# Decode attention beside an MLP: the extra rows of w4 by plain DMAs and h's columns made on chip

## The chip, the cores and the metric

One core of a Trainium2 chip runs the whole program. The metric is the device time of one execution in microseconds (us); lower is better. Before the change it is 403.15 us, the median of 3 runs (402.7 to 404.05).

## The reference

One token (S = 1, D = 1024) goes through a layer norm, then through two branches that are added: attention of 32 query heads over a cache of 65,536 keys in 4 groups, and a mixer with an MLP.

```python
q = (xn @ wq)                                  # 32 heads of 128
p = softmax(q . k * 128 ** -0.5)               # k, v: 4 groups x 65536 x 128, 8 heads share a group
o = (p . v) @ wo
h  = gelu(layernorm(xn) @ w1)
hs = concatenate(shifted quarters of h) @ w2   # S = 1: every shifted quarter is zero
x1 = xn + hs
h2 = gelu(layernorm(x1) @ w3) @ w4             # w3: 1024 x 3584, w4: 3584 x 1024
out = x0 + attention + x1 + h2                 # x0: the token before the layer norm
```

All inputs are bf16. K and V together are 134 MB, and the program reads 170 MB in all.

## The kernel before

**Slots.** Everything large is read into one of three slots of 64 KB per partition, in the order of a list: wq; then K and V of a group in two halves each (a half is 8.4 MB, 64 KB on each of 128 partitions); w3 behind the first K and V; behind the third group a slot with w1, w4's first piece (12 of w4's 25 row blocks) and "x4"; at the end wo, and a last slot with w2 and w4's pieces of 9, 3 and 1 blocks. `ensure(i + LOOKAHEAD)` issues a slot two ahead of the one that is computed on, from SP, as soon as the slot's last user three places earlier is done.

**w4's rows.** w4 has 3584 = 28 x 128 rows. 25 x 128 of them are laid out evenly, 25 rows on each partition (FB = 25). The other 384 rows are "x4" and are not spread evenly: the table XP lists ranges of partitions that get four rows each (eleven ranges, 70 partitions, 280 rows) and ranges that get one row each (five ranges, 104 partitions, 104 rows). Partitions outside of the ranges have zeros there. On a partition the four-row column block comes first (4 x 1024 values, 8 KB), then the one-row block (2 KB).

**How the x4 rows come.** `fill_x_row` (L138) works out, on DVE, a table of one row number for each partition and each of the two blocks; partitions out of the ranges get a number over the bound. `gather_rows` (L155) issues an indirect DMA from GpSimd that reads the row for each partition and skips those over the bound. In `issue`, x4 is zeroed by GpSimd (L167) and filled by two such gathers.

**How h comes.** `compute_w3` (L375) makes h (3584 values) as eight rows of 448 in PSUM, applies gelu on ACT into `hrow` (partitions 0, 32, 64 and 96, two rows each), and calls `bounce` (L360): GpSimd writes the rows to a scratch in DRAM (L363), reads them back as 25 columns with one value for each partition (L367), and, as x4 needs h's values in the very places of its rows, gathers five more columns by the same row tables (L371, L156).

**The product.** `compute_w4(0)` and `compute_x4` add up w4's first piece and x4 in one PSUM tile (`pair_acc`, L526); the result joins the output row through `row_acc` (L230). Each engine has one queue and works it off in order. SP has the queue q1, GpSimd's DMAs are q0, and the sixteen DMA engines serve both.

**K and V.** `compute_K` (L426) transposes a half of K in place on DVE (L435), makes scores on PE (L439), the maxima on DVE, and the exponentials on ACT (L462); `compute_V` (L479) multiplies on PE (L486) and rescales on DVE (L494). The output is copied on ACT (L417) and written from SP (L418).

Of the kernel before, what the change touches and what calls it, by code (L numbers as in the profile page):

```python
# [8 lines left out]
BF16 = mybir.dt.bfloat16  # L9
F32 = mybir.dt.float32  # L10
ACTF = mybir.ActivationFunctionType
ALU = mybir.AluOpType
# [11 lines left out]
XR = (4, 1)  # L24
XP = (((0, 15), (16, 20), (28, 44), (48, 52), (60, 70), (72, 74), (76, 78), (80, 82), (84, 87), (92, 100), (124, 128)),
      ((0, 20), (28, 52), (60, 88), (92, 120), (124, 128)))
NO_ROW = 4096
HEAD = 96


# [1 line left out]
def kernel(  # L32
# [14 lines left out]
    nc = tc.nc  # L47
    P = 128
# [7 lines left out]
    F = B_w3.shape[1]  # L56
    DC = D // P
    FC = F // P
    NOUT = A_wo.shape[1]
# [4 lines left out]
    FW = F // 8  # L64
# [7 lines left out]
    const = ctx.enter_context(tc.tile_pool(name="const", bufs=1))  # L72
# [3 lines left out]
    tpool = ctx.enter_context(tc.tile_pool(name="tp", bufs=2))  # L76
# [3 lines left out]
    ps_M = ctx.enter_context(tc.tile_pool(name="psM", bufs=2, space=bass.MemoryType.PSUM))  # L80
# [5 lines left out]
    FB = sum(W4_PIECES)  # L86
    w4_v = B_w4[0:P * FB, :].rearrange("(m c) n -> m c n", c=FB)
    x_n = [sum(b - a for a, b in r) for r in XP]
    x_start = [P * FB + sum(XR[j] * x_n[j] for j in range(i)) for i in range(len(XR) + 1)]
    assert x_start[-1] == F and all(x_start[i] % r == 0 and F % r == 0 for i, r in enumerate(XR))  # L90
    wo_v = A_wo.rearrange("(p j) n -> p (j n)", p=P)
    w1_v = B_w1.rearrange("(p c) n -> p (c n)", c=DC)
    w2_v = B_w2.rearrange("(m c) n -> m (c n)", c=DC)
# [4 lines left out]
    def source(piece):  # L98
        kind = piece[0]
        if kind == "wq":  # L100
            return wq_v
        if kind == "w3":
            return w3_v
        if kind == "w1":
            return w1_v
        if kind == "w2":
            return w2_v
        if kind == "wo":
            return wo_v
        if kind == "w4":  # L110
            c0 = w4_start[piece[1]]
            return w4_v[:, c0:c0 + W4_PIECES[piece[1]], :].rearrange("p c n -> p (c n)")
        _, g, t, _ = piece
        cache = A_k_cache if kind == "K" else A_v_cache
        return cache[0, g, t * BK:(t + 1) * BK, :].rearrange("(p k) d -> p (k d)", p=P)
# [14 lines left out]
    st = {}  # L130
    loaded = {}


    x_row = []
    for i in range(len(XR)):
        x_row.append(const.tile([P, 1], mybir.dt.uint32, name=f"x_row{i}"))

    def fill_x_row():  # L138
        pi = tmp(1).bitcast(mybir.dt.int32)
        nc.gpsimd.iota(pi, pattern=[[0, 1]], base=0, channel_multiplier=1)  # L140
        pf = tmp(1)
        nc.vector.tensor_copy(out=pf, in_=pi)
        for i, r in enumerate(XR):
            row, step = tmp(1), tmp(1)
            nc.vector.tensor_scalar(out=row, in0=pf, scalar1=float(x_start[i] // r + NO_ROW), scalar2=None, op0=ALU.add)
            end = 0
            for a, b in XP[i]:
                for t, jump in ((a, -NO_ROW - (a - end)), (b, NO_ROW)):
                    nc.vector.tensor_scalar(out=step, in0=pf, scalar1=float(t), scalar2=float(jump),
                                            op0=ALU.is_ge, op1=ALU.mult)  # L150
                    nc.vector.tensor_tensor(out=row, in0=row, in1=step, op=ALU.add)
                end = b
            nc.vector.tensor_copy(out=x_row[i][:], in_=row)

    def gather_rows(i, dst, src):  # L155
        nc.gpsimd.indirect_dma_start(out=dst, out_offset=None, in_=src,  # L156
                                     in_offset=bass.IndirectOffsetOnAxis(ap=x_row[i][:, 0:1], axis=0),
                                     bounds_check=x_start[i + 1] // XR[i] - 1, oob_is_err=False)

    def issue(pieces):  # L160
        t = big.tile([P, SLOT], BF16, name="slot")
        at = 0
        for piece in pieces:
            if piece[0] == "x4":
                w = sum(XR) * NOUT
                loaded[piece] = t[:, at:at + w]
                nc.gpsimd.memset(loaded[piece], 0.0)  # L167
                for i, r in enumerate(XR):
                    gather_rows(i, t[:, at:at + r * NOUT], B_w4.rearrange("(u r) n -> u (r n)", r=r))
                    at += r * NOUT  # L170
                continue
            src = source(piece)
            w = src.shape[-1]
            nc.sync.dma_start(out=t[:, at:at + w], in_=src)
            loaded[piece] = t[:, at:at + w]
            if piece[0] in ("K", "V"):
                for h in range(HALVES):
                    loaded[(piece[0], piece[1], HALVES * piece[2] + h)] = t[:, h * KEYS:(h + 1) * KEYS]
            at += w
        assert at <= SLOT  # L180
# [3 lines left out]
    for a in range(4):  # L184
        nc.scalar.dma_start(out=x_bf[32 * a:32 * a + 32, :],  # L185
                            in_=A_x[0, 0, 32 * a * DC:(32 * a + 32) * DC].rearrange("(p c) -> p c", c=DC))
# [6 lines left out]
    def ensure(upto):  # L193
        while n_issued[0] <= min(upto, len(slots) - 1):
            issue(slots[n_issued[0]])
            n_issued[0] += 1
# [5 lines left out]
    ident_bf = early[:, 0:64].bitcast(BF16)  # L202
# [11 lines left out]
    def tmp(w):  # L214
        n_tmp[0] += w
        assert n_tmp[0] <= 512
        return early[:, n_tmp[0] - w:n_tmp[0]]
    fill_x_row()
    xpad2 = const.tile([P, DC, 32], BF16, name="xpad2")
    nc.gpsimd.memset(xpad2[:], 0.0)  # L220
    qst = const.tile([P, 4 * 520], BF16, name="qst")
# [49 lines left out]
    for j in range(4):  # L271
        accx = tpool.tile([1, QC], F32, name="accx", tag="pT")
        nc.vector.tensor_scalar(out=accx[:], in0=x_row_bf[0:1, QC * j:QC * (j + 1)], scalar1=ln_s1[0:1, 0:1],
                                scalar2=ln_s2[0:1, 0:1], op0=ALU.mult, op1=ALU.add)
# [19 lines left out]
                          in_=sel8[:].unsqueeze(2).to_broadcast([P, 8, 4]))  # L294

    selw = const.tile([P, 2], F32, name="selw")
    for b in range(2):
        nc.vector.tensor_tensor(out=selw[:, b:b + 1], in0=ident_f[:, 32 * b:32 * b + 1],
                                in1=ident_f[:, 64 + 32 * b:64 + 32 * b + 1], op=ALU.add)
# [5 lines left out]
    for b in range(2):  # L305
        for par in range(2):
            nc.vector.tensor_copy(out=psel[:, 2 * b + par, :].rearrange("p (a i) -> p a i", a=4),
                                  in_=iv[:, b, par, :].unsqueeze(1).to_broadcast([P, 4, 32]))


    def rows_product(key, part, wt, xp, width, n_chunks):
        if part == 0:
            st[key] = ps_S.tile([P, 2, 512], F32, name="rows", tag="sc")
        acc = st[key]
        n_c = wt.shape[1]
        for cl in range(n_c):
            c = n_c * part + cl
            for j in range(4):
                for bk in range(2):
                    ch = 4 * bk + j  # L320
                    if ch < n_chunks:
                        nc.tensor.matmul(acc[32 * j:32 * j + 32, bk, 0:width], lhsT=xp[:, c, :],  # L322
                                         rhs=wt[:, cl, ch * width:(ch + 1) * width],
                                         start=(c == 0), stop=(c == DC - 1), tile_position=(0, 32 * j),
                                         skip_group_check=True)
        return acc
# [30 lines left out]
                             skip_group_check=True)  # L357
        nc.vector.tensor_copy(out=qsel[:], in_=pq[:])

    def bounce(rows_ap, view, n, C, tag, extra=False):  # L360
        scr = dram.tile([1, n], BF16, name=f"scr_{tag}")
        flat = scr[0, :]
        nc.gpsimd.dma_start(out=view(flat), in_=rows_ap)  # L363
        dst = const.tile([P, C + (sum(XR) if extra else 0)], BF16, name=f"dst_{tag}")
        if extra:
            nc.gpsimd.memset(dst[:, C:], 0.0)
        nc.gpsimd.dma_start(out=dst[:, 0:C], in_=flat[0:P * C].rearrange("(p c) -> p c", c=C))  # L367
        if extra:
            at = C
            for i, r in enumerate(XR):  # L370
                gather_rows(i, dst[:, at:at + r], flat.rearrange("(u r) -> u r", r=r))  # L371
                at += r
        return dst

    def compute_w3():  # L375
        wt = loaded[("w3",)].rearrange("p (c n) -> p c n", n=F)
        acc = rows_product("psh", 0, wt, xpad2, FW, 8)
        hrow = ppool.tile([P, 2, FW], BF16, name="hrow", tag="p")
        nc.scalar.activation(out=hrow[:], in_=acc[:, :, 0:FW], func=ACTF.Gelu_apprx_tanh)
        st["hT"] = bounce(hrow[:].rearrange("(j u) b n -> j u b n", u=32)[:, 0],  # L380
                          lambda f: f.rearrange("(b j n) -> j b n", b=2, j=4), F, FB, "h", True)

    def compute_w1():
        wt = loaded[("w1",)].rearrange("p (c n) -> p c n", n=D)
# [155 lines left out]
    def compute_wo():  # L540
        wt = loaded[("wo",)].rearrange("p (j n) -> p j n", n=NOUT)
        pair_open(wt.shape[1] + DC)
        for j in range(wt.shape[1]):
            pair_acc(oT[:, j:j + 1], wt[:, j, :])

    compute = {"wq": compute_wq, "w3": compute_w3, "w1": compute_w1, "w2": compute_w2, "w4": compute_w4, "x4": compute_x4,
               "wo": compute_wo, "K": compute_K, "V": compute_V}
    for i, pieces in enumerate(slots):
# [37 lines left out]
```

## Time and profile before

| what | value |
|---|---|
| median of 3 runs | 403.15 us |
| the profiled execution, its time | 402.7 us |
| its span | 400.9 us |
| PE busy | 215.5 us (54%) |
| DVE busy | 220.8 us (55%) |
| ACT busy | 35.7 us (9%) |
| POOL busy | 14.7 us (4%) |
| read from HBM | 170.41 MB, 425 GB/s over the span |
| chain of waits, by engine | DMA 54%, DVE 32%, PE 10% |

The profile is one execution, taken by the hardware profiler. Its times count from the span's start. A row of a timeline gives the start, the busy time, the engine, the line, the operation, what it writes and reads, and in brackets how long the engine had been idle before and what ended that. A name with q behind it (SPq) is that engine's issue of a DMA or a wait of its sequencer. POOL is GpSimd. In a strip of 40 digits each is the busy share of a fortieth of the span in tenths. The trace also has every DMA packet with its queue, size, start and duration, and the moment at which each of the sixteen DMA engines reports its part of a transfer as landed; a packet isn't labelled with its engine.

### The profile page before, as it was taken

The page shows a single profiled execution, that of the slowest core. Times are in us where ns is not written, and L with a number is a line of the kernel's source. Part 1 is how long each engine was busy: PE and PEld are TensorE (multiplying, and loading weights), DVE is VectorE, ACT ScalarE, POOL GpSimd, SP SyncE. Part 2 cuts the span into 40 slices and gives each one's busy share as a digit, 9 for nine tenths or more (in the row PEclk, how much of TensorE's full clock was granted, in tenths as well). Part 3 has the DMA queues.
Part 4 walks back from the last instruction along what each step waited for, and adds up shares of the span by engine and source line. Part 5 has one row for each costly group of instructions (what it writes and reads, how often), then busy time and mean ns, then how long its engine had stood idle before and what let it go on. Part 6 is the DMA issues. An engine that isn't in the chain of part 4 may idle for free.

```text
span 400.9 us, 3470 instructions
## 1 busy us (share of the span) xinstructions
PE 215.5 (54%) x1450; PEld 87.9 (22%) x1450; DVE 220.8 (55%) x319; ACT 35.7 (9%) x62; POOL 14.7 (4%) x24
## 2 busy tenths in 40 slices
PE   0004778630885197409674953395800965295663
PEld 0002223210332032103221321142400422041321
DVE  0007599401986498429846972597503973497300
ACT  0001000500012001100110011001300021001100
POOL 3000000002000000000000004100000000000000
PEclk9999969875698689957955999589865898599757
DMA  9999999999999999999999999999999999999995
GB/s 386 451 419 419 418 420 452 463 427 426 373 446 432 432 426 414 451 432 451 420 438 418 427 458 432 423 427 410 471 419 418 445 438 459 432 419 418 420 416 226
DMA packets 4236, 170.11 MB, mean 424 GB/s; under 512 B 887, under 2 KB 899, under 8 KB 1207
## 3 DMA queue, kind: packets, MB, share of 16 engines
q1 hardware_dynamic: 3608, 169.09, 97.8%
q0 software_dynamic: 416, 0.81, 0.5%
q8 instruction: 11, 0.18, 0.2%
q10 hardware_dynamic: 196, 0.00, 0.0%
q14 instruction: 5, 0.03, 0.0%
HBM read 170.41 MB, written 0.01 MB: 425 GB/s over the span
## 4 chain that ended last, share of the span: by engine, by line
DMA 54%; DVE 32%; PE 10%; another core or an unknown queue 2%; ACT 1%; ACTq 1%; issue 1%; SPq 0%; DVEq 0%
DMA slot<-in_A_k_cache_dram 38%; DVE slot L435 27%; DMA x_row_bf<-in_A_x_dram 9%; DMA slot<-in_B_w_dram 7%; PE oacc L486 4%; PE sc L439 3%; DVE mx L443 3%; PE rows L322 1%; DVE pT L476 1%; PE psB L231 1%; DVE og L494 1%; ACTq L185 0%; PE pm_mx L452 0%; DVE qst L335 0%
## 5 line engine op out<-in xcount | busy, mean ns | idle before, releaser
L439 PE MATMUL sc<-slot,qst 128*128 128x512 bf16 x512 | 136.0, 419 | 100.7 <-DVE slot L435 100.6
L435 DVE STREAM_TRANSPOSE slot<-slot 128x2048 f32<-128x2048 f32 x64 | 142.9, 2280 | 66.4 <-DMA slot<-in_A_k_cache_dram 66.4
L439 PEld LDWEIGHTS <-qst 128*128 128x128 bf16 x512 | 52.1, 104 | 173.0 <-DMA slot<-in_A_k_cache_dram 60.8
L486 PE MATMUL oacc<-slot,pT 128*32 128x512 bf16 x512 | 40.4, 472 | 6.8 <-DVE og L494 3.4
L462 ACT ACTIVATE p_sb<-sc,nm 128x1024 bf16<-128x1024 f32 x16 | 17.8, 1113 | 185.0 <-DVE nm L459 120.7
L476 DVE STREAM_TRANSPOSE pT<-p_sb 128x1024 bf16<-128x1024 bf16 x16 | 19.9, 1244 | 17.3 <-ACT p_sb L462 17.3
L443 DVE TENSOR_REDUCE mx<-sc 128x1 f32<-128x1024 f32 x16 | 19.2, 1203 | 4.5 <-PE sc L439 4.4
L486 PEld LDWEIGHTS <-pT 128*32 128x32 bf16 x512 | 15.4, 112 | 24.9 <-issue 14.0
L494 DVE SCALAR_TENSOR_TENSOR og<-og,alpha,oacc 128x512 f32<-128x512 f32 x12 | 8.8, 735 | 21.6 <-PE oacc L486 21.6
L243 PE MATMUL pm_ln<-early 128*128 128x1 f32 x4 | 1.1, 354 | 33.2 <-DVE early L279 30.6
L237 DVE CAST early<-x_bf 128x8 f32<-128x8 bf16 x1 | 0.2, 172 | 29.0 <-DMA x_bf<-in_A_x_dram 29.0
L445 PE MATMUL pm_mx<-ident_f,mx 128*1 128x128 f32 x16 | 4.3, 270 | 15.9 <-DVE mx L443 15.9
L462 ACT ACT_TABLE_LOAD x3 | 3.8, 1283 | 92.6 <-DVE nm L457 58.0
L167 POOL MEMSET slot<- 128x5120 bf16 x1 | 4.4, 4364 | 148.8 <-PE oacc L486 148.8
L509 PE MATMUL pm_e<-og,sel8q 128*32 128x128 f32 x32 | 6.0, 348 | 5.0 <-DVE og L501 5.0
L243 PEld LDWEIGHTS pm_ln<-early 128*128 128x128 f32 x4 | 1.0, 311 | 33.2 <-issue 30.6
L452 PE MATMUL pm_mx<-ident_f,rep 1*128 1x1 f32 x16 | 3.6, 226 | 8.1 <-DVE rep L449 8.1
L530 PE MATMUL pm_w<-slot,oT 128*1 128x512 bf16 x64 | 6.0, 557 | 3.3 <-DMA slot<-in_A_wo_dram 3.3
L452 PEld LDWEIGHTS pm_mx<-ident_f,rep 1*128 1x128 f32 x16 | 2.3, 142 | 18.2 <-DVE rep L449 18.2
L445 PEld LDWEIGHTS pm_mx<-ident_f,mx 128*1 128x1 f32 x16 | 1.3, 79 | 21.2 <-DVE mx L443 20.4
L509 PEld LDWEIGHTS pm_e<-og,sel8q 128*32 128x32 f32 x32 | 4.1, 139 | 8.3 <-DVE og L501 7.8
L322 PE MATMUL rows<-slot,xpad 128*32 128x448 bf16 (+1 forms) x80 | 5.5, 358 | 0.0
(101 smaller groups left out, 100.1 us busy)
## 6 DMA issues: line engine op xcount, KB each, us to landing
slot<-in_B_w_dram SPq DMA_DIRECT2D x1, 7168.0 KB, 33.0
slot<-in_B_w_dram SPq DMA_DIRECT2D x2, 2048.0 KB, 28.4
slot<-in_B_w_dram SPq DMA_DIRECT2D x1, 3072.0 KB
slot<-in_B_w_dram SPq DMA_DIRECT2D x1, 2304.0 KB, 27.1
slot<-in_B_w_dram SPq DMA_DIRECT2D x1, 768.0 KB
slot<-in_B_w_dram SPq DMA_DIRECT2D x1, 256.0 KB
slot<-in_A_k_cache_dram SPq DMA_DIRECT2D x8, 48.6
slot<-in_A_v_cache_dram SPq DMA_DIRECT2D x8, 37.3
```

Of the source, the lines that this page charges most:

```text
L322: nc.tensor.matmul(acc[32 * j:32 * j + 32, bk, 0:width], lhsT=xp[:, c, :], rhs=wt[:, cl, ch * width:(ch + 1) * width], start=(c == 0), sto ...
L435: nc.vector.transpose(out=kf[:, cg, :], in_=kf[:, cg, :])
L439: nc.tensor.matmul(sc[:, hf, :], lhsT=qst[:, o:o + 128], rhs=kr[:, cg, hf, :, bp // 2, :, bp % 2], start=(cg == 0 and bp == 0), stop=(cg = ...
L443: nc.vector.reduce_max(out=mx[:], in_=sc[:].rearrange("p h n -> p (h n)"), axis=AX.X)
L445: nc.tensor.transpose(pm[0:1, 0:P], mx[:, 0:1], ident_f[:])
L452: nc.tensor.transpose(pm[:, P:P + 1], rep[0:1, :], ident_f[0:1, 0:1])
L462: nc.scalar.activation(out=p_sb[:], in_=sc[:], func=ACTF.Exp, bias=nm[:, 0:1], scale=SCALE, accum_out=lb[:, 0:1])
L476: nc.vector.transpose(out=pT[:], in_=p_sb[:])
L486: nc.tensor.matmul(oacc[32 * u:32 * (u + 1), :], lhsT=pT[:, hf, 32 * t:32 * (t + 1)], rhs=vt[:, :, hf, t, :], start=(hf == 0 and t < 4), s ...
L494: nc.vector.scalar_tensor_tensor(out=st["og"][:], in0=st["og"][:], scalar=alpha[:, 0:1], in1=oacc[:], op0=ALU.mult, op1=ALU.add)
L509: nc.tensor.matmul(pe[rows, 0:P], lhsT=sel8q[:], rhs=og[:, 128 * cg:128 * (cg + 1)], start=(cg == 0), stop=(cg == 3), tile_position=(0, 32 ...
L530: nc.tensor.matmul(psW[32 * q:32 * q + 1, :], lhsT=lhsT, rhs=wrow[:, 512 * b:512 * b + 512], start=(i < 2), stop=(i >= n - 2), tile_positi ...
```

## The change

The sixteen ranges of XP are read by sixteen plain DMAs from GpSimd, one for each range, into the same places of the slot. The row tables, their computation on DVE and the gathers go. h's five extra columns no longer come from DRAM: one partition (96) of `hrow` holds the last 448 values of h, and all 384 that x4 needs are among them. DVE copies them, range by range, into a zeroed row `hx` of five times 128 values, in the order of the partitions; PE turns each of the five into a column by a matmul with one partition and a 1 x 1 identity; DVE copies the five columns behind the 25 of the tile that the read-back fills. `bounce` keeps its two DMAs.

```diff
-NO_ROW = 4096
...
-    def fill_x_row():
-        pi = tmp(1).bitcast(mybir.dt.int32)
-        nc.gpsimd.iota(pi, pattern=[[0, 1]], base=0, channel_multiplier=1)
...
-    def gather_rows(i, dst, src):
-        nc.gpsimd.indirect_dma_start(out=dst, out_offset=None, in_=src,
-                                     in_offset=bass.IndirectOffsetOnAxis(ap=x_row[i][:, 0:1], axis=0),
-                                     bounds_check=x_start[i + 1] // XR[i] - 1, oob_is_err=False)
...
                 nc.gpsimd.memset(loaded[piece], 0.0)
                 for i, r in enumerate(XR):
-                    gather_rows(i, t[:, at:at + r * NOUT], B_w4.rearrange("(u r) n -> u (r n)", r=r))
+                    row = x_start[i]
+                    for a, b in XP[i]:
+                        nc.gpsimd.dma_start(out=t[a:b, at:at + r * NOUT],
+                                            in_=B_w4[row:row + r * (b - a), :].rearrange("(p r) n -> p (r n)", r=r))
+                        row += r * (b - a)
                     at += r * NOUT
...
-    fill_x_row()
...
-    def bounce(rows_ap, view, n, C, tag, extra=False):
+    def bounce(rows_ap, view, n, C, tag, extra=0):
...
-        if extra:
-            nc.gpsimd.memset(dst[:, C:], 0.0)
         nc.gpsimd.dma_start(out=dst[:, 0:C], in_=flat[0:P * C].rearrange("(p c) -> p c", c=C))
-        if extra:
-            at = C
-            for i, r in enumerate(XR):
-                gather_rows(i, dst[:, at:at + r], flat.rearrange("(u r) -> u r", r=r))
-                at += r
         return dst
...
+        n_x, last = sum(XR), slice(96, 97)
+        hx = tpool.tile([P, n_x, P], BF16, name="hx", tag="pT")
+        nc.vector.memset(hx[last], 0.0)
+        first = 0
+        for i, r in enumerate(XR):
+            at = x_start[i] - (F - FW)
+            for a, b in XP[i]:
+                nc.vector.tensor_copy(out=hx[last, first:first + r, a:b].rearrange("q r p -> q p r"),
+                                      in_=hrow[last, 1, at:at + r * (b - a)].rearrange("q (p r) -> q p r", r=r))
+                at += r * (b - a)
+            first += r
+        ph = ps_M.tile([P, 512], F32, name="pm_hx", tag="pm")
+        for r in range(n_x):
+            nc.tensor.matmul(ph[:, r:r + 1], lhsT=hx[last, r, :], rhs=ident_bf[last, 96:97], start=(r == 0),
+                             stop=(r == n_x - 1), tile_position=(96, 0), skip_group_check=True)
+        nc.vector.tensor_copy(out=st["hT"][:, FB:FB + n_x], in_=ph[:, 0:n_x])
```

More of the change, by code (lines that the diff above doesn't have):

```diff
@@ L89 @@
     x_start = [P * FB + sum(XR[j] * x_n[j] for j in range(i)) for i in range(len(XR) + 1)]
-    assert x_start[-1] == F and all(x_start[i] % r == 0 and F % r == 0 for i, r in enumerate(XR))
+    assert x_start[-1] == F and x_start[0] >= F - FW and all(x_start[i] % r == 0 and F % r == 0 for i, r in enumerate(XR))
     wo_v = A_wo.rearrange("(p j) n -> p (j n)", p=P)
@@ L131 @@
     loaded = {}
-    x_row = []
-    for i in range(len(XR)):
-        x_row.append(const.tile([P, 1], mybir.dt.uint32, name=f"x_row{i}"))
-    def fill_x_row():
-        pi = tmp(1).bitcast(mybir.dt.int32)
-        nc.gpsimd.iota(pi, pattern=[[0, 1]], base=0, channel_multiplier=1)
-        pf = tmp(1)
-        nc.vector.tensor_copy(out=pf, in_=pi)
-        for i, r in enumerate(XR):
[L144 to L153, printed above, removed]
-    def gather_rows(i, dst, src):
-        nc.gpsimd.indirect_dma_start(out=dst, out_offset=None, in_=src,
-                                     in_offset=bass.IndirectOffsetOnAxis(ap=x_row[i][:, 0:1], axis=0),
-                                     bounds_check=x_start[i + 1] // XR[i] - 1, oob_is_err=False)
     def issue(pieces):
@@ L363, in bounce @@
         nc.gpsimd.dma_start(out=view(flat), in_=rows_ap)
-        dst = const.tile([P, C + (sum(XR) if extra else 0)], BF16, name=f"dst_{tag}")
-        if extra:
-            nc.gpsimd.memset(dst[:, C:], 0.0)
+        dst = const.tile([P, C + extra], BF16, name=f"dst_{tag}")
         nc.gpsimd.dma_start(out=dst[:, 0:C], in_=flat[0:P * C].rearrange("(p c) -> p c", c=C))
-        if extra:
-            at = C
-            for i, r in enumerate(XR):
-                gather_rows(i, dst[:, at:at + r], flat.rearrange("(u r) -> u r", r=r))
-                at += r
         return dst
@@ L380, in compute_w3 @@
         st["hT"] = bounce(hrow[:].rearrange("(j u) b n -> j u b n", u=32)[:, 0],
-                          lambda f: f.rearrange("(b j n) -> j b n", b=2, j=4), F, FB, "h", True)
+                          lambda f: f.rearrange("(b j n) -> j b n", b=2, j=4), F, FB, "h", sum(XR))
+        n_x, last = sum(XR), slice(96, 97)
[14 more added lines that the diff above has]
+        nc.vector.tensor_copy(out=st["hT"][:, FB:FB + n_x], in_=ph[:, 0:n_x])
     def compute_w1():
```

## The prediction

> **What bounds the kernel.** I read the page's slices and queues first, then the chain of waits, then the transfers' issues, then single packets and landings.
>
> ```profile
> DMA  9999999999999999999999999999999999999995
> ...
> q1 hardware_dynamic: 3608, 169.09, 97.8%
> q0 software_dynamic: 416, 0.81, 0.5%
> q8 instruction: 11, 0.18, 0.2%
> ```
>
> The sixteen DMA engines are busy in every slice but the last, nearly all of it with SP's queue (q1). GpSimd's queue (q0), which the change touches, has 0.5%: 0.005 x 401 = 2 us per engine. The chain of waits ends so:
>
> ```profile
> 368.41 28.46 DMA slot<-in_B_w_dram
> 396.87 0.04 issue
> 396.91 1.05 PE psB L231 x14
> 397.96 0.02 issue
> 397.99 0.37 ACT out L417
> ```
>
> The end is the landing of the last weights and 3.4 us behind it (397.5 to the span's 400.9). SP's issues show that the data never runs out:
>
> ```profile
> 276.26 0.33 SPq L174 DMA_DIRECT2D slot<-in_A_k_cache_dram  x1
> ...
> 291.02 0.33 SPq L174 DMA_DIRECT2D slot<-in_A_k_cache_dram  x1
> ...
> 367.56 1.75 SPq L174 DMA_DIRECT2D slot<-in_B_w_dram  x4
> ```
>
> What was queued ahead of these three had landed in full only at 288.1 (w4's first piece), 326.8 (V) and 384.8 (wo): the issues are 12, 36 and 17 us early. The time is therefore the work of whichever DMA engine is slowest, and I count per engine.
>
> **Per engine.** Each transfer of q1 is split alike over the sixteen engines, and each engine reports its own landing. Sorted, in us:
>
> ```
> w4's first piece  285.5 285.5 285.7 286.5 287.2 287.2 287.2 287.2 287.2 287.4 287.5 287.6 287.7 287.7 287.9 288.1
> wo                382.1 383.7 383.8 383.8 383.8 383.9 383.9 384.0 384.1 384.2 384.3 384.4 384.5 384.6 384.7 384.8
> last piece of w4  396.4 396.4 396.6 396.6 396.6 396.6 396.7 396.8 396.9 397.0 397.1 397.2 397.3 397.4 397.5 397.5
> ```
>
> The gathers are uneven. The r = 4 gather of h's columns (8-byte rows) shows seven packets of 64 B, so seven engines hold eight such rows each; the other 14 of the 70 are on six engines. The r = 1 gather shows thirteen packets of 16 B. Three engines hold none: in the w4 gathers they show 4-byte placeholders instead (255.999, 256.013, 256.288, and again every 2.42 us, eight times). These are the three that land first at 285.5 to 285.7. They lose their lead later. Code comes in eleven 16-KB packets on q8, of 0.88 to 0.97 us each, and the 64-KB packet next to one takes about 2.9 us instead of 2.42: 1.4 us in all. The loads at 336.1, 374.5 and 390.7 each coincide with one leader falling back. So the empty placement on three engines pays for code loads there, and at the end all sixteen arrive within 1.1 us. By this reading the three arrive at the front of that band; which place an engine has in a sorted row isn't labelled, and other executions may differ by tenths, so between 0 and 1.1 us ahead of the last I take 0.7.
>
> **Part 1: sixteen plain DMAs for two gathers into the slot.** Bytes are the same; what moves is who carries them. The trace has four plain GpSimd DMAs. h's eight rows to DRAM come as four packets of 1,792 B, h's mixed-in row as two of 1,024 B on two engines, the 128-partition reads as sixteen packets of 400 and of 128 B: each is spread over as many engines as it has outer rows, in even shares. I take it that the ranges are spread so too, from wherever each one begins. Then an engine gets 384/16 = 24 rows of 2 KB on average. The share can't be quite even: 70 four-row partitions are 4.4 per engine, so some engine has five (20 rows), and 104 single rows in pairs are 3.25 per engine, so some has four pairs (8 rows): 28 at most if the starts rotate. I take 26. Price: an 8-KB packet took 309 ns, so 77 ns a row: 26 x 0.077 = **+2.0 us** on the three engines that had none. Bounds: 0 (each row stays where the gather had it) and 53 rows, 4.1 us (an engine takes part in every range).
>
> The Trainium skill (DMA: Bandwidth & Descriptors, section on why a DMA increments its semaphore by 16) says that a plain transfer uses the largest number of engines up to 16 that divides its outer size, consecutive ones from a rotating cursor. By that rule the three get 22 to 26 rows, whatever the start, an estimate of 1.7 to 2.0 us. The trace's two packets on two engines agree with its count; where the cursor stands, no run here shows.
>
> **Part 2: the packets' turns.** q0 and q1 take turns packet by packet: placeholders return every 2.42 us, one 64-KB packet (2,418 ns) apart. A plain DMA takes two turns on every engine: for h's rows, 88.784 and 91.205 on an engine that carries nothing. Sixteen make 32 turns, against 18 on the three empty engines now (eight placeholders and an end for each gather). A 4-byte packet takes 9 ns, about 12 with its gap: 14 x 12 ns = **+0.2 us** of engine time. POOL's issues:
>
> ```profile
> 246.03 4.36 POOL L167 MEMSET slot<- 128x5120 bf16 x1 [148.85 <-PE oacc L486]
> 250.67 1.00 POOL L156 DMA_INDIRECT slot<-in_B_w_dram,x_row  x1 [0.27 <-POOL slot L167]
> 251.98 1.00 POOL L156 DMA_INDIRECT slot<-in_B_w_dram,x_row  x1 [0.30 <-issue]
> ```
>
> Plain ones took 0.58 to 0.76 us, so sixteen with gaps of 0.3 are 14 to 17 us: 250.7 to about 267, ahead of POOL's next duty at 284.74. With first packets near 254.8, 27 turns pass by 287 (eight packets and an end for each of V's, w1's and w4's transfers), and the last five cost 2.42 each: the rows land at about 300, against 278.8. Waiting for them: PE's x4 products, behind them K's at 309.85, and SP's refill of that slot (291.02, now about 303). Cover: 9 us ahead of PE, 23 us ahead of an empty queue (326). Cost 0; GpSimd's next transfers queue behind them, but are wanted only at 390.
>
> **Part 3: h's columns on chip.** Removed: two gathers of 8- and 2-byte rows. The landings around them (97.55 mean, then 117.96; the next pair is 19.4 apart) lose 1.0 us on average. The three latest, 98.2, 99.0 and 99.2, plus 19.4 give 117.6, 118.4 and 118.6 against a last three of 118.3, 118.7 and 118.9: 0.3 lost at least on whichever were late. Bounds for the three empty engines 0 and 1.0; I take **-0.3 us**, as they carry placeholders only. Added: a memset, sixteen one-partition copies and a PSUM copy on DVE, five small matmuls. A one-row copy took at most 0.40 us (L273, 256 columns): 18 x 0.4 = 7 us at most, from 84.5.
>
> ```profile
> 99.19 2.31 DVE L435 STREAM_TRANSPOSE slot<-slot 128x2048 f32<-128x2048 f32 x1 [17.89 <-DMA slot<-in_A_k_cache_dram]
> ```
>
> They lie in this wait of 17.89 us; PE idles too. Without cover they would cost those 7 us. The columns' copy needn't wait for the row DMA into the same tile: the gather at 94.78 didn't wait for the one issued at 93.89.
>
> **Part 4: x_row's fill goes**, some 70 DVE instructions of 0.14 us up to 44.6. They fill gaps beside the x transfer (39.38); saved on the path 0.07. Nothing, since data bounds.
>
> **Sum.** The three engines change by 2.0 + 0.2 - 0.3 = +1.9 us, of which the 0.7 of slack costs nothing: their last landing is 397.5 + 1.2 = 398.7, **+1.2 us**. The other thirteen gain 1.0 from part 3; seven go from 40 rows to about 24 (-1.2), six from 16 to 20 up to about 24 (+0.6 at most): none ends later than now. The profiled execution took 402.7, the runs' median is 0.45 above it: 403.15 + 1.2 = **404.4** (case A). Without slack and with 28 rows it is +2.1, 405.2; with 1.1 of slack, 24 rows and 0.6 gained, +0.3, 403.4: A's own range. A lies on the bound of 0.3% (1.2 us), about what a measurement of this kernel can tell from no change.
>
> **Rivals.**
>
> B, rows stay on their engines. For: the ranges are the same partitions. Against: h's rows from four partitions went over four engines. Then the thirteen gain 1.0 less 0.2 and the three stay at 396.4: 397.5 - 0.8, so **402.4**. The Trainium skill (same page, section on the descriptor swizzle) ties engines to partitions for full transfers; if it held for short ranges this would be the outcome, and no run here shows it.
>
> C, the rows come too late; this is the slower side. Three or more turns per DMA (rows cut in two, or POOL slowed while DVE transposes from 255 to 276) give 48 turns: 287 + 21 x 2.42 = 338. It decides from about 310, when PE's in-order stream holds K's products; DVE's wait of 7 us at 338.8 absorbs the first part. Landing at 338 holds K's scores 28 us, V's 21 us behind that, and the chain to wo's products (oT ready 382.5, wo at 384.8) slips by 10 or so: **410** (405 to 414). Against: two turns seen in all four plain DMAs.
>
> D, the small gathers cost every engine 1.0, the empty ones too, and the rows' spread falls on engines with slack: -1.0 -0.3 = **401.8**. Against: the late three lost 0.3.
>
> **How the numbers follow.** A 0.67, B 0.12, C 0.11, D 0.10. A's value is the bound itself; the slack is its least known term, and I give the smaller slacks slightly more than half: slower 0.36, same 0.31. B: same 0.08, faster 0.04. C: slower 0.11. D: faster 0.08, same 0.02. Together faster 0.12, same 0.41, slower 0.47. Range 402.0 to 406.2: it holds A and B whole, and D's edge and C's mildest end.
>
> **What would show it.** Three engines last by 1 us or more at the end, and no longer first after w4's first piece: A. All sixteen spread as now: B. PE's x4 products after 310 and K's behind them: C. The interval from 97 to 118 shortened to about 19.5 supports part 3. A queue that runs empty anywhere, or DVE delayed past 99.2, would make the whole reading wrong.

## The result and the profile after

The changed kernel takes **410.89 us** (median of 6 runs, 410.01 to 411.52), the kernel before 403.66 us (median of 6, 402.7 to 404.35). The ratio is 1.0181, 95% interval 1.0164 to 1.0198: slower by 7.2 us, where 404.4 was predicted. The profiled executions were 402.7 before and 411.52 after, the lowest and the highest of their runs, so the traces differ by 8.8 us.

Of the page of the changed kernel, the strips of the DMA engines' busy share and of what they moved, and the queue of GpSimd (packets, MB, share of 16 engines):

```profile
DMA  9999999999999999999999999999999999999993
GB/s 410 410 410 410 505 394 448 395 463 442 416 422 424 473 417 429 416 473 411 441 410 469 410 448 418 356 334 356 397 408 435 423 422 430 461 429 418 421 413 140
...
q0 software_dynamic: 640, 0.81, 0.6%
```

The engines are as busy as before, yet they moved less in the 26th to 29th slices: 356, 334, 356, 397 GB/s between 256 and 297 us (before: 423, 427, 410, 471). The sixteen DMAs are issued from 250.24 us on, and the last of their rows is in at 308.9. The same thing by stretches; the columns are the stretch, its length, busy time of PE, PEld, DVE, ACT and POOL, PE's granted clock, the busy share of the DMA engines, and GB/s. First before:

```profile
200.00:250.00 50.00, 30.63 (x208) 12.38 (x208) 31.72 (x39) 4.56 (x9) 3.96 (x1) 0.79 1.00 434
252.00:277.00 25.00, 17.68 (x66) 6.92 (x66) 20.11 (x13) 1.39 (x3) 0.97 (x1) 0.77 0.98 420
277.00:302.00 25.00, 10.77 (x134) 4.81 (x134) 7.97 (x21) 3.85 (x6) 1.19 (x2) 0.77 1.04 449
310.00:380.00 70.00, 45.27 (x269) 18.10 (x268) 48.09 (x43) 7.23 (x13) 0.00 (x0) 0.84 1.00 433
```

Then after:

```profile
200.00:250.00 50.00, 31.12 (x208) 12.27 (x207) 29.99 (x35) 4.57 (x9) 4.37 (x1) 0.80 1.00 432
252.00:277.00 25.00, 16.91 (x66) 6.73 (x66) 21.41 (x15) 1.39 (x3) 3.77 (x8) 0.83 0.96 352
277.00:302.00 25.00, 14.28 (x124) 5.46 (x124) 6.82 (x19) 3.26 (x5) 3.13 (x6) 0.64 1.03 370
310.00:380.00 70.00, 39.58 (x212) 15.53 (x216) 46.60 (x37) 6.03 (x11) 0.57 (x1) 0.82 1.00 434
```

Only the two middle rows differ in GB/s (352 for 420, 370 for 449), at a busy share that is the same to 0.02. Busy engines that move less have slower packets. Of the 64-KB packets that start between 252 and 270 us, the median takes 2,418 ns before and 2,674 ns after (mean 2,422 and 2,834), and 80% take over 2,450 ns instead of 1%. That is more than a conflict with one engine each could explain: from 250 to 274 us there are 134 64-KB packets and 40 of 8 KB, each of which lasts about an eighth as long. Had every 8-KB packet held up one other engine, it would have met one 64-KB packet there, at times two, so some 45 of the 134; 94 took over 2,450 ns.

The chain of waits shows the consequence (start, length, what). The rows that were expected at 300 are in at 308.9, and the refill of their slot moves to 309.63:

```profile
253.77 30.52 DMA slot<-in_B_w_dram
...
284.56 24.35 DMA slot<-in_B_w_dram
...
309.63 45.19 DMA slot<-in_A_k_cache_dram
...
376.83 26.89 DMA slot<-in_B_w_dram
```

This chain looks like a late transfer that pushes the end. The landings say otherwise. Mean over the sixteen engines, and the last, in us:

```
                        before            after
V of group 1, second    117.96            117.00      (-1.0)
K of group 3, second    253.61            252.58      (-1.0)
w4's first piece        287.06            292.40      (+5.3)
K of group 4, first     306.56            313.28      (+6.7)
V of group 4, first     325.86            332.60      (+6.7)
wo                      384.03            390.68      (+6.7)
last piece of w4        396.91 / 397.5    403.53 / 406.2
```

From 313 on nothing more is lost: K, V, K, V and wo follow each other 19.3 to 19.4 us apart as before, so no queue ran dry and the late rows cost nothing by being late. The account of the 8.7 us between the last landings is: -1.0 up to 118, +7.7 between 252 and 313, and +2.1 because the last engine is 2.65 us behind the mean instead of 0.58.

Two things went otherwise than described without mattering for the end. GpSimd's timeline (columns as in a timeline before):

```profile
250.24 4.03 POOL L143 DMA_DIRECT2D slot<-in_B_w_dram  x8 [0.29 <-POOL slot L139]
260.97 0.51 POOL L143 DMA_DIRECT2D slot<-in_B_w_dram  x1 [6.71 <-DMA slot<-in_B_w_dram]
267.63 0.50 POOL L143 DMA_DIRECT2D slot<-in_B_w_dram  x1 [6.14 <-DMA slot<-in_B_w_dram]
```

Eight DMAs go out at once; each further one waits until one of the earlier ones has landed. And DVE:

```profile
103.83 0.17 DVE L367 CAST dst_h<-pm_hx 128x5 bf16<-128x5 f32 x1 [13.30 <-DMA dst_h<-scr_h]
103.91 8.88 DVE L421 STREAM_TRANSPOSE slot<-slot 128x2048 f32<-128x2048 f32 x4
```

The copy of the five columns does wait for the read-back into the same tile, and K's transposes behind it start at 103.91 instead of 99.19.

### The profile page after: what moved, and what is told of

It is laid out like the page before. It is cut to its first block, busy times and chain, and to the rows that moved or that the text cites. A ratio compares the mean times of both kernels' runs of the same rounds, so it can differ in the third digit from the quotient of the medians.

```text
span 409.7 us, 3449 instructions
## 1 busy us (share of the span) xinstructions
PE 220.5 (54%) x1455; PEld 88.9 (22%) x1455; DVE 217.0 (53%) x268; ACT 35.7 (9%) x62; POOL 18.5 (5%) x34
## 4 chain that ended last, share of the span: by engine, by line
DMA 63%; DVE 22%; PE 9%; POOL 2%; ACT 1%; issue 1%; ACTq 1%; SPq 0%; DVEq 0%
DMA slot<-in_B_w_dram 28%; DMA slot<-in_A_k_cache_dram 22%; DVE slot L421 17%; DMA x_row_bf<-in_A_x_dram 9%; PE oacc L472 3%; PE rows L297 3%; DMA scr_h<-hrow 2%; DMA dst_h<-scr_h 2%; DVE mx L429 2%; DVE pT L462 1%; PE sc L425 1%; POOL slot L139 1%; PE psB L206 1%; ACT p_sb L448 1%; POOL slot L143 1%
## 5 line engine op out<-in xcount | busy, mean ns | idle before, releaser
L472 PE MATMUL oacc<-slot,pT 128*32 128x512 bf16 x512 | 42.4, 489 | 5.4 <-DVE og L480 2.3
L516 PE MATMUL pm_w<-slot,dst_h 128*1 128x512 bf16 x34 | 4.2, 624 | 15.6 <-DMA slot<-in_B_w_dram 15.6
L143 POOL DMA_DIRECT2D slot<-in_B_w_dram x16 | 8.1, 509 | 27.0 <-DMA slot<-in_B_w_dram 26.7
L297 PE MATMUL rows<-slot,xpad 128*32 128x448 bf16 (+1 forms) x80 | 7.5, 469 | 2.3 <-DMA slot<-in_B_w_dram 2.3
L495 PE MATMUL pm_e<-og,sel8q 128*32 128x128 f32 x32 | 4.2, 276 | 4.7 <-DVE og L487 4.7
```

Of the source, the lines that this page charges most:

```text
L143: nc.gpsimd.dma_start(out=t[a:b, at:at + r * NOUT], in_=B_w4[row:row + r * (b - a), :].rearrange("(p r) n -> p (r n)", r=r))
L472: nc.tensor.matmul(oacc[32 * u:32 * (u + 1), :], lhsT=pT[:, hf, 32 * t:32 * (t + 1)], rhs=vt[:, :, hf, t, :], start=(hf == 0 and t < 4), s ...
L516: nc.tensor.matmul(psW[32 * q:32 * q + 1, :], lhsT=lhsT, rhs=wrow[:, 512 * b:512 * b + 512], start=(i < 2), stop=(i >= n - 2), tile_positi ...
```

## The experiments

The theory after reading the trace, called "places" below: the sixteen DMAs slow all traffic because their engines write into partitions which, in the large transfers, other engines write at the same time. Rivals: the h half has a share; plain GpSimd DMAs or their number do it; the short reads of w4 do it.

| run | what carries the 384 rows | h's columns | us, median | ratio to before (95%) | median 64-KB packet at 252 to 270, ns |
|---|---|---|---|---|---|
| before | two gathers | gathered | 403.66 | | 2,418 |
| after | sixteen DMAs of 2 to 28 partitions | on chip | 410.89 | 1.0181 (1.0164 to 1.0198) | 2,674 |
| e1_h_alone | two gathers | on chip | 402.29 | 0.9970 (0.9957 to 0.9983) | 2,418 |
| e2_x4_alone | the sixteen DMAs | gathered | 412.79 | 1.0226 (1.0197 to 1.0255) | 2,533 |
| e3_one128 | one DMA, 128 partitions | on chip | 402.93 | 0.9982 (0.9968 to 0.9995) | 2,418 |
| e4_four32 | four DMAs of 32 partitions | on chip | 408.04 | 1.0112 (1.0086 to 1.0138) | 2,775 |
| e5_two64 | two DMAs of 64 partitions | on chip | 408.35 | 1.0104 (1.0082 to 1.0126) | 3,036 |
| e6_four128 | four DMAs, 128 partitions, quarter columns | on chip | 403.02 | 0.9980 (0.9969 to 0.9991) | 2,418 |
| e7_to_dram | gathers, and the sixteen again into DRAM | on chip | 404.43 | 1.0020 (1.0010 to 1.0030) | 2,418 |
| e8_even28 | part of w4's first piece, from SP | read back | 402.90 | 0.9975 (0.9964 to 0.9985) | 2,418 |
| e9_third64 | one of 128 (two rows), two of 64 (one row) | on chip | 404.47 | 1.0022 (1.0009 to 1.0035) | 2,418 |
| e10_two64_sp | two DMAs of 64 partitions, from SP | on chip | 406.28 | 1.0060 (1.0043 to 1.0077) | 2,418 |

Each ratio is to runs of the kernel before on the same chip (medians of 403.5 to 403.8). e1 to e4 ran on one chip, e5 to e8 on a second, e9 and e10 on a third, so a difference between runs of two chips is good to some 0.3 us. In e9 and e10 the partial DMAs (those over a part of the 128 partitions) run behind 270 us, and in e7 the DMAs into DRAM run from 4 to 79 us, out of the last column's stretch.

### The two halves

e1_h_alone takes h's half of the change and keeps `fill_x_row` and the gathers for w4; against the changed kernel:

```diff
-                    row = x_start[i]
-                    for a, b in XP[i]:
-                        nc.gpsimd.dma_start(out=t[a:b, at:at + r * NOUT],
-                                            in_=B_w4[row:row + r * (b - a), :].rearrange("(p r) n -> p (r n)", r=r))
-                        row += r * (b - a)
+                    gather_rows(i, t[:, at:at + r * NOUT], B_w4.rearrange("(u r) n -> u (r n)", r=r))
```

> The h half alone: h's columns on chip, w4's rows by the two gathers as before. Theory: this half is a small gain, the 1.0 us that the small gathers cost thirteen engines between 97 and 118 us; the late three gain 0.3, so the time is 0.3 to 1.0 us under before, ratio 0.9975 to 0.9995. The strip of GB/s has no dip at 256 to 297 us. Rival: DVE's copy, which now waits 13.3 us for the read-back, costs at the end too; then the time is 1 us or more over before.

Measured 402.29: 1.4 us under the 403.7 of its own runs of before, more than the 1.0 that was expected at most, though the ratio's interval reaches into the expected range. The mean landing after the small gathers' place is 117.03 for 117.96; the three latest there are at 117.5, 118.2 and 118.3 for 118.3, 118.7 and 118.9. DVE's copy waits here too (11.70 us, K's transposes at 104.97) and costs nothing.

e2_x4_alone is the kernel before with the sixteen DMAs in place of the two gathers for w4.

> The w4 half alone: sixteen plain DMAs for w4's rows, h's columns still gathered. Theory: the whole loss and more sits here: after's +7.2 us plus the 1.0 that the h half gives, so +8 us, ratio 1.020 (1.017 to 1.023), with the dip to 330 to 360 GB/s at 256 to 297 us. Rival: the two halves share the loss; then under +6 us.

Measured 412.79, +9.1 us, within the expected ratio. Its two stretches:

```profile
252.00:277.00 25.00, 16.34 (x64) 6.67 (x65) 19.25 (x12) 0.64 (x1) 6.82 (x12) 0.80 0.99 373
277.00:302.00 25.00, 14.48 (x128) 5.59 (x125) 8.98 (x21) 4.01 (x8) 3.13 (x6) 0.70 1.04 365
```

The dip comes with w4's DMAs alone (365 to 373 GB/s). So the h half is a gain (1.4 us in e1, 1.9 between e2 and the changed kernel), and the loss sits whole in w4's half.

### Partitions, number, bytes

From here on every partition gets three extra rows, so the transfers can have regular shapes:

```diff
-XR = (4, 1)
-XP = (((0, 15), (16, 20), (28, 44), (48, 52), (60, 70), (72, 74), (76, 78), (80, 82), (84, 87), (92, 100), (124, 128)),
-      ((0, 20), (28, 52), (60, 88), (92, 120), (124, 128)))
+XR = (3,)
+XP = (((0, 128),),)
```

That is e3_one128. In e4_four32 XP is `(((0, 32), (32, 64), (64, 96), (96, 128)),)`, in e5_two64 `(((0, 64), (64, 128)),)`.

> Three extra rows on each of 128 partitions, so one plain GpSimd DMA over all partitions; h's columns on chip. Every engine carries 24 rows, into the partitions that it serves in every other transfer. Theory (places: the loss comes from engines that write into partitions which another engine serves): no dip, only the unevenness of code loads against equal rows: +0.4 to +2.1 us over before, 404.1 to 405.8. Rival (plain GpSimd DMAs as such slow the traffic, in proportion to their bytes): the same bytes, so a dip as in after and +6 us or more.

> The same three rows on each partition as in the run with one DMA, but by four plain DMAs of 32 partitions each, so that an engine gets two neighbouring partitions of each and nearly all writes fall on partitions that another engine serves in the large transfers. Theory (places): a dip as in after, +4 to +8 us over the run with one DMA. Rival (number of DMAs): four of sixteen, so a quarter of after's 7.6 us at most, +2 us over the run with one DMA.

e3: 402.93, under the kernel before and under the expected 404.1, so the theory was right on the dip and set the unevenness too high. Every engine now has 24 rows, the very share that had been priced as the loss, and there is no dip; the time is 0.6 us over e1, which ran on the same chip. The unevenness is there but small: the last engine is 1.69 us behind the mean, against 0.99 in e1, whose rows are placed unevenly.

e4: 408.04, +5.1 over e3 with the same bytes, shares and issuer. The stretch that holds its four DMAs, first e3, then e4:

```profile
252.00:277.00 25.00, 17.29 (x66) 6.90 (x66) 20.51 (x15) 1.39 (x3) 0.00 (x0) 0.79 0.97 418
```

```profile
252.00:277.00 25.00, 17.65 (x66) 6.97 (x66) 20.14 (x13) 1.39 (x3) 0.00 (x0) 0.77 0.96 346
```

418 against 346 GB/s. That leaves the cut in partitions and the number of DMAs as causes; e6 keeps the number and takes the cut away:

```diff
+                        src = B_w4[row:row + r * (b - a), :].rearrange("(p r) n -> p (r n)", r=r)
+                        w4th = r * NOUT // 4
+                        for q in range(4):
+                            nc.gpsimd.dma_start(out=t[a:b, at + q * w4th:at + (q + 1) * w4th],
+                                                in_=src[:, q * w4th:(q + 1) * w4th])
```

> Three rows on each partition by two plain DMAs of 64 partitions; an engine gets four neighbouring partitions of each, and by the split of the large transfers half of them are its own. Theory (places): half of what the four DMAs of 32 partitions lost against one DMA (5.1 us), so +2 to +3.5 us over the run with one DMA, 405 to 406.5, with a shallower dip. Rival (number of DMAs beyond one, linear): one extra against three, +1.7 us at most, and the run with four full DMAs then loses 5.

> The same rows by four plain DMAs, each over all 128 partitions and a quarter of the columns (1.5 KB). Four DMAs, as in the run that lost 5.1 us, but every engine writes its own partitions. Theory (places): no dip, within 0.7 us of the run with one DMA, 402.3 to 403.7. Rival (number of DMAs): +5 us, 408.

e6: 403.02, the same as one DMA, packets at 2,418 ns. The number is out:

```profile
252.00:277.00 25.00, 16.65 (x66) 6.63 (x66) 21.18 (x15) 1.39 (x3) 0.00 (x0) 0.85 0.95 407
```

(407 against e3's 418 says nothing: the undisturbed kernels have 407 to 420 in this stretch.) e5 is a miss: 408.35, +5.4, where half a loss was expected, and its packets are slowed more than e4's (3,036 ns). So a transfer over 64 of the 128 partitions is as bad as one over 32. The loss doesn't follow the share of misplaced writes as I had worked it out.

e9 varies the bytes, `XR = (2, 1)` with `XP = (((0, 128),), ((0, 64), (64, 128)))`:

> Two of the three rows by one plain DMA over 128 partitions, the third by two plain DMAs of 64 partitions: the partial DMAs move a third of the bytes that they moved in the run with two DMAs, which lost 5.4 us against one DMA. Theory (the loss goes with the bytes that partial DMAs write): a third, +1.8 us over 402.93, 404.7 (404.1 to 405.4). Rival (it goes with the number of partial DMAs): +5.4 us, 408.

404.47, +1.5 over e3, where a third of e5's loss is 1.8 and the whole is 5.4. The same two partial DMAs with a third of the bytes lose about a third, so their number is out and the bytes count. They are also in flight for a shorter time: from 271 to 280 us, beside w1's 16-KB packets (a median of 747 ns for e3's 611), where e5's ran from 251 to 280, for the most part beside 64-KB packets. So e9 alone doesn't part the bytes from the time in flight.

### Reads or writes

e7 adds to e1 the sixteen DMAs of the change with a scratch in DRAM as their target:

```diff
+                scr_x = dram.tile([F, NOUT], BF16, name="scr_x")
+                for i, r in enumerate(XR):
+                    row = x_start[i]
+                    for a, b in XP[i]:
+                        nc.gpsimd.dma_start(out=scr_x[row:row + r * (b - a), :].rearrange("(p r) n -> p (r n)", r=r),
+                                            in_=B_w4[row:row + r * (b - a), :].rearrange("(p r) n -> p (r n)", r=r))
+                        row += r * (b - a)
```

> The kernel with h's columns on chip and the gathers (402.29) plus sixteen more plain GpSimd DMAs that read the same ranges of w4 once more and write them to a scratch in DRAM that nobody reads, with the same pieces and the same spread over engines as in after. Theory (places in SBUF): the reads and the turns do no harm by themselves; 0.79 MB more cost their own time, 24 to 28 rows an engine, +1.5 to +3.5 us with the writes, and 64-KB packets near 2.42 us. Rival (the short, near reads of w4 by many engines at once slow HBM): the dip of after, +7 us or more and 64-KB packets of 2.7 to 2.9 us.

404.43, +2.1 over e1 for 0.79 MB of more reads and as many writes. GpSimd issues these DMAs not beside the gathers at 252 us but at the program's start:

```profile
4.17 4.04 POOL L174 DMA_DIRECT2D scr_x<-in_B_w_dram  x8
...
44.43 0.49 POOL L174 DMA_DIRECT2D scr_x<-in_B_w_dram  x1 [2.13 <-DMA scr_x<-in_B_w_dram]
```

They run beside wq, K, V and w3, the last one landing at 79 us, so the stretch from 252 us says nothing about them. The stretch from 10 to 60 us does, first e1, then e7:

```profile
10.00:60.00 50.00, 19.27 (x115) 7.88 (x116) 23.06 (x120) 2.39 (x4) 0.00 (x0) 0.93 0.99 425
10.00:60.00 50.00, 18.01 (x113) 7.60 (x114) 21.13 (x119) 2.39 (x4) 3.90 (x8) 0.97 1.04 446
```

No dip: of e7's 316 64-KB packets that start between 12 and 60 us the median takes 2,418 ns and three take over 2,450. What is paid is about the time of the DMAs' own bytes (384 rows at 77 ns over sixteen engines are 1.85 us), and it is paid early: V of group 1, second, lands at 118.92 for e1's 117.03. The packets are cut otherwise than in the changed kernel, though: each DMA is split into sixteen equal packets (the one of 120 KB into sixteen of 7,680 B), so e7 repeats the number and the bytes of the DMAs, and not their pieces or their spread over engines as was expected. For the reads e3, e4 and e5 are the closer comparison: all three read the same rows in 128 packets of 6 KB from GpSimd's queue, and e3 has no dip. With both, the reads as such are out, and what is left is where a partial DMA's engines write in SBUF; that last step is inferred.

### From SP, and without extra rows

e10 is e5 with `nc.sync.dma_start` in place of `nc.gpsimd.dma_start`.

> The two DMAs of 64 partitions as in the run that lost 5.4 us, issued from SP instead of GpSimd, so they stand in the same queue as the large transfers, behind w4's first piece, and take no turns between 64-KB packets. Theory (a partial DMA writes partitions that another engine is writing at the same moment): what is left is the short stretch in which the pieces themselves collide, 1.85 us of transfer made up to twice as long, so +0 to +2.5 us over 402.93, 402.9 to 405.4, and 64-KB packets of 2.42 us before and after. Rival (partial DMAs slow everything however they are queued): +5 us, 408.

406.28, +3.4: between the two expectations. The trace shows where: up to 282 us the packets are as before; then for about 6 us, while the two DMAs run, their own 6-KB packets take 301 to 535 ns on average in each 2 us (a median of 234 ns in e3), w4's 24-KB packets up to 1.7 us for 0.91, and K's 64-KB packets up to 4.8 us; from 292 all is as before. A partial DMA hurts only while it runs, from SP too; in GpSimd's queue, where its packets take turns with 64-KB ones, that is 28 us, and the loss is 5.4. Beside e9, whose partial DMAs run for a similar time with a third of these bytes and lose 1.5, the bytes count at a like time in flight; beside e5, the same bytes lose less in a shorter time. So neither alone sets the loss.

e8 drops x4: `W4_PIECES = (15, 9, 3, 1)`, and 28 columns of h are read back.

> No extra rows at all: w4 laid out evenly, 28 rows on each partition, all from SP, so the first piece has 15 rows instead of 12; no row tables, no GpSimd DMAs for w4, no columns made on chip. Theory: the three rows cost what they cost in the run with one GpSimd DMA, as every engine has 24 rows in its own partitions: 402.5 to 403.5, ratio to before 0.997 to 1.000. Rival: uneven placement that pays for code loads is worth more than 1 us, so 1 us or more over before.

402.90, as expected. The uneven placement of 384 rows by gathers, with h's columns on chip (e1, 402.29), is 0.6 us ahead of this far simpler kernel in the medians, but the two ran on different chips and their ratios to before, 0.9970 and 0.9975, have overlapping intervals, so a gain isn't shown.

## Why the prediction was wrong

**The bound** was read rightly: the time is what the DMA engines need, no engine's arithmetic decides, and none of the late waits in the changed kernel reached the end.

**Part 1 failed.** "Bytes are the same; what moves is who carries them", priced at 77 ns a row on the engine that carries it: +2.0 us. The price took a packet's time on its own engine for its whole cost. Into SBUF, by partial DMAs, the 384 rows cost all sixteen engines 7.7 us more than the gathers did: 16 x 7.7 = 123 us of engine time for 384 x 0.077 = 30 us of transfer, four times as much on top of it. The spread itself was taken nearly rightly (after has 70 packets of four rows, 50 of two and 4 of one). The term that was meant, unevenness, exists: equal shares leave the last engine 1.7 us behind the mean in e3, 1.0 in e1, and cost 0.6 us between these two; it was 2.1 us more in after than before. So +1.2 was the right order for the smaller of two effects. That the rows would leave their engines was a step of the prediction; what it does to the other engines when a row is written from a new one was the next question, and I didn't ask it. The gathers of the trace, whose 8-KB packets left the 64-KB packets at 2,418 ns (all but one, beside a code load), couldn't warn: by the sizes of their packets, with eight four-row partitions on seven engines and none on three, they seem to keep each partition to one engine.

The Trainium skill (DMA: Bandwidth & Descriptors, section on the descriptor swizzle) gives the rule that was cited for rival B: in a transfer over 128 partitions each engine writes a fixed set of partitions of its own. The runs agree with it as far as they go: e3 and e6 (whole transfers) leave the 64-KB packets at 2,418 ns, e4 and e5 (parts) lose 5 us. The same page (section on back-pressure in remote DMA) says that a saturated SBUF port holds up the sending engine and others that share its path. It says so for transfers between cores; that all engines' packets are slowed alike here would fit, and no run shows that this is the mechanism.

**Part 2**: the turns were right (the sixteen DMAs leave 388 packets of 4 bytes on q0, an end on each of the sixteen engines and a placeholder on those that carry none of a DMA's rows); the landing was 309 for 300, with two causes at hand that weren't parted: GpSimd had only eight DMAs in flight (26.7 us of waits at L143), and all packets were slower. The cover held: PE's x4 products ended at 309.6, K's began at 318.57, itself late by the slower transfers.

**Part 3**: right in sign and low in size: -0.3 was taken for the late engines, e1 gives -1.4 in the median and -0.6 between the last landings of the two traces (396.9 for 397.5). The step that the columns' copy needn't wait was wrong (13.30 us), the cover that I named for the DVE work, an idle wait for data, was eaten by it, and the queue hid the rest: the next load that hung on it went out at 125.12, 12 us ahead of the last landing of what was queued (137.6). By the prediction's own sign a DVE delayed past 99.2 would have made the whole reading wrong; it was delayed to 103.91 at no cost, so that sign was too strict.

**Part 4**: nothing, as said.

**Rivals.** C named the rows' lateness, with a time near the measured one, but its mechanism isn't what happened: the rows were in at 309, before its deciding point, and e3, e6 and after's landings behind 313 show no cost of lateness. B and D described the gain of the h half only.

**Open.** No record says which engine wrote which partition, so "another engine's partitions" is inferred from the shapes that hurt (64, 32 and fewer partitions into SBUF) and those that don't (128 partitions; DRAM). That all engines write at once into the few partitions of one part, whichever engine serves these otherwise, would fit as well, and no run parts the two. Why halves hurt as much as quarters isn't settled either, nor why a byte of a partial DMA costs about two (e10) to four times (the change) its own time on top of it.

## What to carry to other kernels

When DMA engines bound a kernel, price a transfer by what it does to the others, not only by its bytes: a part of the partitions, written while full transfers run, cost two to four times its own time on top of it here. Keep small loads in the shape of the large ones (all 128 partitions, fewer columns), even if there are more of them. A chain of waits that runs through a late transfer isn't proof that lateness costs; compare the landings behind it.

## What the runs showed of the hardware

- 64-KB packets, 2,418 ns almost without exception, took a median of 2.5 to 3.0 us while partial transfers into SBUF were in flight from GpSimd (in e4 every one of 90 took over 2,540 ns), and 2,418 ns beside sixteen DMAs of the same rows into DRAM.
- Four DMAs over 128 partitions cost no more than one (403.02 and 402.93); two over 64 cost 5.4 us.
- Gathers of 8-byte and 2-byte rows cost the engines about 1.0 us each on average (mean landings of 117.96 with and 117.03 without), although they moved 768 bytes.
